# Linear attention and a squared-ReLU FFN on one core: the first phase is issued from a written table instead of by the scheduler

## The chip, the cores and the metric

The kernel runs on one core of a Trainium2 chip. The metric is device time in microseconds (us). The kernel before was run three times: 893.98, 896.58 and 896.88 us, median 896.58. The profile is of one more execution, which took 896.0 us; the span that the profile covers is 894.0 us.

## What is computed

Eight batches of eight heads, 576 positions, head size 64. In each head, q is normalised by a softmax over the head size and k by a softmax over the positions; the output is q times (k transposed times v). The outputs of the heads of one position stand side by side as 512 columns, and a feed-forward network follows.

```python
def _attn_ref(q, k, v):
    q_s = q - np.max(q, axis=-1, keepdims=True)
    q_s = np.exp(q_s)
    q_s = q_s / (np.sum(q_s, axis=-1, keepdims=True) + 1e-09)
    k_s = k - np.max(k, axis=2, keepdims=True)
    k_s = np.exp(k_s)
    k_s = k_s / (np.sum(k_s, axis=2, keepdims=True) + 1e-09)
    kv = np.einsum('bhsd,bhse->bhde', k_s, v)
    return np.einsum('bhsd,bhde->bhse', q_s, kv).astype(np.float32)

def _moe_ref(x, w_in, w_out):          # x: 4608 x 512
    h = x @ w_in                       # 512 x 2048, float64
    r = np.maximum(h, 0.0)
    return ((r * r) @ w_out).astype(np.float32)   # 2048 x 512, float64
```

## The kernel before, in words

**Work.** Heads go in pairs, four pairs to a batch, 32 pairs in all; I call them pair 0 to pair 31. The 576 positions of a batch are 512 that make a block of the FFN and 64 that are left over; the left-overs of all eight batches make a ninth block. So the FFN has nine blocks of 512 rows. A block has 16 chunks of 128 FFN columns. For each chunk the kernel forms h (`ffn_h`, L427: four parts over the 512 input columns, each three matmuls of 512 columns, L407 to L409, because every operand is split into a high and a low half), applies ReLU and the square and splits the result (`activate`, L411), and two steps later adds the chunk's product with w_out to four accumulators (`ffn_out`, L433: four parts of three matmuls, L441 to L443).

**Weights.** They arrive as float64, 512 KB a chunk, 16 chunks of w_in and 16 of w_out. `load_w` (L144) fetches one on SP's queue; `split_weight` (L153) turns it into a float32 high and low half: two ACT operations (L165 on the lowest byte, L167 into PSUM bank 3), two on DVE (L169, L170), one more on ACT (L177) and one on POOL (L178). All 32 chunks go through the same PSUM bank, one after the other.

**Attention of the first two batches** (pairs 0 to 7, the early form). Per pair: the maximum of k (L219), its transpose on PE (L223), a second maximum (L225) and its spread over the partitions (L251); k minus this, exponential (L256, L257); the same for q with a maximum per row (L261, L263, L266), its sum and division (L273 to L276); k times v on PE (L300), scaled (L308 to L316); q transposed on PE (L348, L350), copied (L353); the product (L359), split into x_hi and x_lo (L189, L190). Pairs 8 to 31 use another form, which transposes q through a bounce in DRAM (L285, L288).

**What sets the order.** The program is written unit by unit (L479 to L579): loads in the order of `LOADS` (L31), attention of batch 0 in a skewed loop (L498), h parts of the first four chunks as pairs finish, then block 0 with the attention of batch 1 in numbered slots. The framework's scheduler then decides the order on every engine from its own estimates, steered by `tc.high_priority` and `tc.issue_after`. Once built, each engine executes its own list strictly in order, and an instruction waits on semaphores of other engines or of transfers. SP issues the loads, except for q of pairs 0 and 1, which ACT issues.

**Buffers.** Four PSUM banks (`banks`) serve all uses; four more are the first phase's own (`ps_first`, L92) and later the accumulators (`ps_o`, L515). k, v and q tiles of pairs 0 to 3 are separate; from pair 4 on they share two sets (`NB = 2`, L69).

Of the kernel before, what the change touches and what calls it, by code (L numbers as in the profile page):

```python
# [42 lines left out]
def attention_ffn_kernel(ctx: ExitStack, tc: tile.TileContext, q, k, v, w_in, w_out, out):  # L43
# [48 lines left out]
    ps_first = start.enter_context(tc.tile_pool(name="ps_first", bufs=2, space=bass.MemoryType.PSUM))  # L92
# [42 lines left out]
    def load_one(b, pr, n):  # L135
        load(tiles(b, pr)[n], (k, q, v)[n], b, pr, n)

    def load_pair(b, pr):
        for n in range(3):
            load_one(b, pr, n)  # L140

    chunks, last = [], []
# [10 lines left out]
    def split_weight(part, fc):  # L153

        raw = raws[part, fc]
        low, high = raw[:, :, 0], raw[:, :, 1]
        w = w_pool.tile([P, 512], U32, name="w", bufs=WB)
        wf = w.bitcast(F32)

        with ExitStack() as order:
            if his:
                order.enter_context(tc.issue_after(his[-1].ins))
            nc.scalar.activation(low, raw.bitcast(U8)[:, :, 3], AF.Copy, scale=1 / 32, bias=-15.5 / 32)  # L165
        t = banks[3]
        nc.scalar.activation(t, high.bitcast(F32), AF.Copy, scale=2.0**-112)  # L167
        t = t.bitcast(U32)
        nc.vector.scalar_tensor_tensor(out=t, in0=t, scalar=3, in1=low, op0=ALU.logical_shift_left, op1=ALU.bitwise_or)  # L169
        nc.vector.scalar_tensor_tensor(out=w, in0=high, scalar=0x80000000, in1=t, op0=ALU.bitwise_and, op1=ALU.bitwise_or)  # L170
        finish_split()
        chunk = stay.tile([P, 2, 512], F32R, name=f"w{part}{fc}", tag=f"{part}{fc}")
        chunks.append(chunk)
        (wi if part == "i" else wo)[fc] = chunk

        def parts():
            his.append(nc.scalar.copy(chunk[:, 0], wf))  # L177
            nc.gpsimd.tensor_tensor(chunk[:, 1], wf, chunk[:, 0].bitcast(F32), op=ALU.subtract)  # L178

        unsplit.append(parts)  # L180

    his, unsplit = [], []

    def finish_split():
        while unsplit:
            unsplit.pop()()

# [4 lines left out]
    def ordered(f, *args):  # L192

        with ExitStack() as order:
            if last:
                order.enter_context(tc.issue_after(last[-1].ins))
            return f(*args)

    def attention(b, pr):

        n = b * NPAIR + pr
        i = n % NB
        kk, qq, vv = tiles(b, pr)
        kvd = kvn[i]
        early = n < EARLY
        e_q = nc.gpsimd if early else nc.vector
        st = {}
        odd = early and n % 2 == 1

        def bank(cols):  # L210
            if b == 0 and odd:
                t = ps_first.tile([P, NT], F32, name="first_ps", tag="a")
            else:
                t = next_bank("first" if b == 1 else "a") if b else banks[2]
            return t[:, :cols]

        def k_max():
            m = attn_pool.tile([P, 2, D], F32, name="m")
            nc.vector.tensor_reduce(m, kk.rearrange("p h j d -> p h d j"), axis=AX.X, op=ALU.max)  # L219
            if early:  # L220

                ps = bank(2 * P) if b else ps_first.tile([P, 2 * P], F32, name="max_ps", tag="a")
                last.append(nc.tensor.transpose(ps[:, :P], m.rearrange("p h d -> p (h d)"), ident))  # L223
                st["mc"] = attn_pool.tile([P, 1], F32, name="mc", bufs=2)
                nc.vector.tensor_reduce(st["mc"], ps[:, :P], axis=AX.X, op=ALU.max)  # L225
                st["mb"] = ps
                if b == 0:
                    k_spread()
            else:


                mt = attn_pool.tile([P, 4, BLK], F32, name="mt", bufs=1)
                nc.vector.transpose(mt, m.rearrange("p h (e a) -> p (h e) a", a=BLK))
                m1 = attn_pool.tile([P, 4], F32, name="m1", bufs=1)
                nc.vector.tensor_reduce(m1, mt, axis=AX.X, op=ALU.max)
                m4 = attn_pool.tile([BLK, 4, 4], F32, name="m4", bufs=1)
                for g in range(4):
                    nc.vector.tensor_copy(m4[:, g], m1[g * BLK : (g + 1) * BLK])  # L238
                m5 = attn_pool.tile([P, 4, 1], F32, name="m5", bufs=1)
                for g in range(4):  # L240
                    nc.vector.tensor_reduce(
                        m5[g * BLK : (g + 1) * BLK, :, 0], m4.rearrange("p g c -> p c g"), axis=AX.X, op=ALU.max
                    )
                mb = attn_pool.tile([P, 2, 1, D], F32, name="mb", bufs=1)
                nc.vector.tensor_copy(mt, m5.broadcast_to([P, 4, BLK]))
                nc.vector.transpose(mb.rearrange("p h o (e a) -> p (h o e) a", a=BLK), mt)
                st["mb"] = mb

        def k_spread():
            ps = st["mb"]  # L250
            last.append(nc.tensor.matmul(ps[:, P:], st["mc"].broadcast_to([P, P]), ident, start=True, stop=True))  # L251
            st["mb"] = ps[:, P:].rearrange("p (h o d) -> p h o d", h=2, o=1)
# [37 lines left out]
        def kv():  # L290
            ke = st["ke"]
            ps = bank(D + 1)
            for part in range(1 if b else 2):
                for j in range(LOW):
                    for h in range(2):
                        if b:
                            dst, rhs = ps[half[h], : D + 1], vv[:, h, j, :]
                        else:
                            dst, rhs = (ps[half[h], D : D + 1], ones) if part else (ps[half[h], :D], vv[:, h, j, :])
                        mm = nc.tensor.matmul(dst, ke[:, h, j, :], rhs, start=(j == 0), stop=(j == HIGH))  # L300
                        if not b:
                            continue
                        if h == 1 and j == HIGH:
                            last.append(mm)
            if b == 0 and pr < NB:
                pad_v(pr, nc.gpsimd)
# [29 lines left out]
        def q_t_early(j0, j1):  # L336
            def go():
# [13 lines left out]
                if b:  # L351
                    last.append(mm)
# [58 lines left out]
    def activate(ps, blk, fc):  # L411
# [9 lines left out]
        if blk == 0:  # L421
            his.append(gh)
# [187 lines left out]
```

## Time and profile before

| | us |
|---|---|
| runs (three) | 893.98, 896.58, 896.88; median 896.58 |
| the profiled execution | 896.0 |
| its span | 894.0 |
| PE busy in the span | 867.6 (97%) |
| DVE, ACT, POOL busy | 578.2, 408.0, 202.6 |
| first matmul of the FFN starts | 26.82 |
| as many FFN parts are done as block 0 has (64 of h, 64 of output) | 153.7 |

The span starts with the first instruction on the chip. PE's busy time counts a matmul at any clock. The granted clock is 1.00 at 2.4 GHz and 0.50 at 1.2 GHz. In a timeline row, the bracket at the end is the idle time of that engine just before the row, and what ended it. PE idles for 26.4 us of the span; what happens between 26.8 and 153.7 us, the time of block 0, is shown in the rows.

### The profile page before, as it was taken

The numbers are of one execution on the slowest core, as the hardware profiler recorded it, in microseconds if no ns is written. First come the engines' busy times: TensorE is split into PE (matmuls) and PEld (weight loads), VectorE is DVE, ScalarE is ACT, GpSimd is POOL, SyncE is SP. The second block draws the span as 40 slices with busy tenths as digits, with TensorE's granted clock in tenths as the row PEclk, the third lists the DMA queues.
The fourth block names the chain that finished last, engine by engine and source line by source line (L and its number), as shares of the span: only waits on it lengthen the run. The fifth ranks groups of instructions, "written<-read, shape, count | busy, mean of one in ns | idle before, by whom it ended". The sixth has DMA issues, their size and how long they took to land.

```text
span 894.0 us, 12672 instructions
## 1 busy us (share of the span) xinstructions
PE 867.6 (97%) x4368; PEld 702.2 (79%) x4368; DVE 578.2 (65%) x1177; ACT 408.0 (46%) x801; POOL 202.6 (23%) x177
## 2 busy tenths in 40 slices
PE   4899899999999999999999999999999999999997
PEld 3577677888888888878888888888888888888885
DVE  7768798877778776878687768886864342223222
ACT  3867766445444444554454544444444232222222
POOL 3667534222213220231122212222222000000000
PEclk9989999999999999999999999999999999999999
DMA  9897212422142313322322233222411030002001
GB/s 255 269 361 207 69 28 59 118 73 84 44 118 74 82 59 98 92 72 69 92 79 79 57 82 92 79 63 63 101 32 32 3 94 1 1 1 47 1 1 47
DMA packets 95743, 73.18 MB, mean 82 GB/s; under 512 B 47552, under 2 KB 85440, under 8 KB 95680
## 3 DMA queue, kind: packets, MB, share of 16 engines
q1 hardware_dynamic: 94944, 71.53, 28.6%
q10 hardware_dynamic: 736, 0.85, 0.4%
q8 instruction: 34, 0.56, 0.3%
q14 instruction: 29, 0.24, 0.1%
HBM read 54.00 MB, written 18.35 MB: 81 GB/s over the span
## 4 chain that ended last, share of the span: by engine, by line
PE 85%; DVE 3%; DMA 1%; issue 1%; ACT 0%; SPq 0%; DVEq 0%; ACTq 0%
PE o_ps L441 14%; PE o_ps L443 14%; PE o_ps L442 14%; PE bank L407 14%; PE bank L409 13%; PE bank L408 13%; PE bank L300 2%; PE bank L379 1%; DVE w L170 1%; DVE bank L169 0%; DVE r L417 0%; DMA kt<-in_k_dram 0%; DMA qt<-in_q_dram 0%; DVE m L219 0%; DVE m L238 0%
## 5 line engine op out<-in xcount | busy, mean ns | idle before, releaser
L407 PE MATMUL bank<-x_hi,wi 128*128 128x512 f32 x568 | 225.7, 398 | 3.0 <-ACT x_hi L189 2.2
L441 PE MATMUL o_ps<-wo,g_hi 128*128 128x512 f32 x576 | 227.4, 397 | 0.8 <-ACT g_hi L420 0.8
L442 PE MATMUL o_ps<-wo,g_hi 128*128 128x512 f32 x576 | 225.3, 391 | 0.0
L443 PE MATMUL o_ps<-wo,g_lo 128*128 128x512 f32 x576 | 224.4, 391 | 0.0
L409 PE MATMUL bank<-x_hi,wi 128*128 128x512 f32 x568 | 222.9, 392 | 0.0
L408 PE MATMUL bank<-x_lo,wi 128*128 128x512 f32 x568 | 222.6, 392 | 0.0
L419 DVE TENSOR_TENSOR r<-r 128x512 f32<-128x512 f32 x128 | 111.7, 873 | 117.2 <-ACT r L413 116.9
L424 DVE TENSOR_TENSOR g_lo<-r,g_hi 128x512 fp32r<-128x512 f32 x132 | 99.7, 755 | 105.1 <-ACT g_hi L420 102.9
L420 ACT CAST g_hi<-r 128x512 fp32r<-128x512 f32 x144 | 89.3, 620 | 129.6 <-PE o_ps L442 80.1
L413 ACT ACTIVATE r<-bank 128x512 f32<-128x512 f32 x142 | 84.6, 596 | 100.1 <-PE bank L409 95.5
L407 PEld LDWEIGHTS bank<-x_hi,wi 128*128 128x128 f32 x568 | 107.0, 189 | 27.6 <-ACT x_hi L189 3.6
L441 PEld LDWEIGHTS o_ps<-wo,g_hi 128*128 128x128 f32 x576 | 108.4, 188 | 24.3 <-ACT g_hi L420 1.0
L443 PEld LDWEIGHTS o_ps<-wo,g_lo 128*128 128x128 f32 x576 | 108.6, 188 | 22.5
L442 PEld LDWEIGHTS o_ps<-wo,g_hi 128*128 128x128 f32 x576 | 108.6, 189 | 22.3 <-POOL wo L178 0.2
L409 PEld LDWEIGHTS bank<-x_hi,wi 128*128 128x128 f32 x568 | 107.2, 189 | 23.0
L408 PEld LDWEIGHTS bank<-x_lo,wi 128*128 128x128 f32 x568 | 107.3, 189 | 21.5 <-issue 0.2
L390 POOL TENSOR_TENSOR x_lo<-xf,x_hi 128x256 fp32r<-128x256 f32 x48 | 39.5, 823 | 372.9 <-ACT x_hi L389 372.1
L333 POOL TENSOR_TENSOR qs<-qT,qs 64x640 fp32r<-64x640 f32 x48 | 82.1, 1710 | 58.4 <-ACT qs L332 47.0
L219 DVE TENSOR_REDUCE m<-kt 128x128 f32<-128x640 f32 x32 | 41.5, 1299 | 18.9 <-DMA kt<-in_k_dram 18.9
L332 ACT CAST qs<-qT 64x640 fp32r<-64x640 f32 x48 | 34.9, 726 | 37.1 <-DMA qT<-bounce 36.5
L266 ACT ACTIVATE qn<-qn 128x640 f32<-128x640 f32 x32 | 23.6, 739 | 53.5 <-DVE qn L263 46.5
L381 ACT COPY xf<-bank 64x320 f32<-64x320 f32 (+1 forms) x96 | 37.9, 394 | 20.2 <-PE bank L379 12.0
(118 smaller groups left out, 774.0 us busy)
## 6 DMA issues: line engine op xcount, KB each, us to landing
out_dram<-o SPq DMA_DIRECT2D x70, 128.0 KB, 2.3
raw_i<-in_moe_w_in_dram SPq DMA_DIRECT2D x16, 512.0 KB, 8.3
raw_o<-in_moe_w_out_dram SPq DMA_DIRECT2D x16, 512.0 KB, 9.0
bounce<-tb SPq DMA_DIRECT2D x24, 320.0 KB, 2.1
qT<-bounce SPq DMA_DIRECT2D x96, 80.0 KB, 2.2
kt<-in_k_dram SPq DMA_DIRECT2D x32, 160.0 KB, 2.9
qt<-in_q_dram SPq DMA_DIRECT2D x30, 160.0 KB, 2.9
vt<-in_v_dram SPq DMA_DIRECT2D x56, 80.0 KB, 2.5
```

The lines of the kernel that those rows point to most:

```text
L219: nc.vector.tensor_reduce(m, kk.rearrange("p h j d -> p h d j"), axis=AX.X, op=ALU.max)
L333: nc.gpsimd.tensor_tensor(qs[other], qT[own], qs[own].bitcast(F32), op=ALU.subtract)
L407: nc.tensor.matmul(ps, wi[fc][:, 0, sl], xh[:, cc, :], start=(cc == 0), stop=False)
L408: nc.tensor.matmul(ps, wi[fc][:, 0, sl], xl[:, cc, :], start=False, stop=False)
L409: last.append(nc.tensor.matmul(ps, wi[fc][:, 1, sl], xh[:, cc, :], start=False, stop=(cc == NCC - 1)))
L413: nc.scalar.activation(r, ps, AF.Relu)
L419: nc.vector.tensor_tensor(r, r, r, op=ALU.mult)
L420: gh = nc.scalar.copy(g_hi, r)
L424: e.tensor_tensor(g_lo, r, g_hi.bitcast(F32), op=ALU.subtract)
L441: nc.tensor.matmul(acc[t], g_hi[:, ts], wo[fc][:, 0], start=(n == 0), stop=False)
L442: nc.tensor.matmul(acc[t], g_hi[:, ts], wo[fc][:, 1], start=False, stop=False)
L443: prev = nc.tensor.matmul(acc[t], g_lo[:, ts], wo[fc][:, 0], start=False, stop=(n == NFC - 1))
```

## The change

The first phase, that is all loads, the attention of pairs 0 to 7, all weight chunks, block 0 of the FFN and the first half of pair 8's attention, is no longer written as loops and left to the scheduler. It is a list of 708 tokens, `FIRST`, which is issued word by word with the scheduler switched off (`tc.manual_schedule()`); every engine gets its instructions in the order of this one list. The blocks from 1 on are issued and scheduled as before, in the same slots.

A token names one operation: `Lk0a` is the first of two loads of k of pair 0 (`Lv4a` to `Lv4d` the four of v in pairs from 4 on), `Wi4` the load of chunk 4 of w_in, `wli4 wti4 wci4 wdi4 whi4 wpi4` the six steps of its split (ACT L165, ACT L167, DVE L169, DVE L170, ACT L177, POOL L178 of the kernel before), `H1.0` part 0 of h of chunk 1 (three matmuls), `r1 sq1 gh1 gl1` its activation, `O1.0` part 0 of its output. `m T mc S ks ke`, `qm qs qe sm sa rc qn`, `KV rs kn`, `TA TB ca cb`, `PX PL xh xl lf St` are the steps of a pair's attention; `@B2` or `@C0` names the PSUM bank. `X0` to `X5` are the six first steps of pair 8.

```diff
-EARLY_SPLITS = [("o",2),("o",3),("i",4),("o",0)]
-OFFSET = 100
-LOADS = "k0 q0 v0 k1 q1 v1 k2 q2 w0 v2 k3 q3 v3 w1 w2 w3".split()
-ACT_LOADS = {(0, 0, 1), (0, 1, 1)}
+ACT_LOADS = {0, 1}
+FIRST = """
+Lk0a Lq0b Lk0b Lq1a Lk1a Lq0a Lq1b Lv1b Lk1b Lk2a Lv0a m0 Lv1a Lk2b qm0 T0@C0 Lk3b mc0 Lv0b qs0 qm1 S0 Lq2b m1 Wi0
...
+O13.1 gl14 who15 O13.2 wpo15 O13.3 O14.0 gh15 O14.1 gl15 O14.2 O14.3 O15.0 O15.1 O15.2 O15.3
+""".split()
...
-    ps_first = start.enter_context(tc.tile_pool(name="ps_first", bufs=2, space=bass.MemoryType.PSUM))
+    ps_o = ctx.enter_context(tc.tile_pool(name="ps_o", bufs=4, space=bass.MemoryType.PSUM))
...
+            if name == "W":
+                load_w(part, fc)
+            elif name == "wl":
+                nc.scalar.activation(low, raw.bitcast(U8)[:, :, 3], AF.Copy, scale=1 / 32, bias=-15.5 / 32)
+            elif name == "wt":
+                nc.scalar.activation(t, high.bitcast(F32), AF.Copy, scale=2.0**-112)
...
+            if name == "H":
+                h_part(ps, 0, fc, n)
+            elif name == "r":
+                nc.scalar.activation(new(fc, "r", [P, NT], pool=work), ps, AF.Relu)
...
+        for token in FIRST:
+            if token[0] == "X":
+                steady[0][0][int(token[1:])]()
+                continue
+            name, n, part, bank = re.fullmatch(r"([A-Za-z]+)(\d+)(\.\d|[a-d])?(?:@(\w+))?", token).groups()
...
+    with tc.manual_schedule():
+        first_phase()
+    tc.no_sync_barrier()
+
+    steps = [(blk, fc) for blk in range(B + 1) for fc in range(NFC)]
...
-    for n in range(len(steps) + LAG):
+    for n in range(NFC, len(steps) + LAG):
```

The numbers of instructions by engine and kind are the same in both programs. Three places where the order differs follow; the line numbers of the second list of each are those of the changed kernel.

PE, from the pair products to the first h matmuls. `first_ps`, `early` and `bank` are PSUM tiles, `vt` and `ke` v and the exponential of k, `qT` and `qe` q transposed, `wi` a split chunk of w_in. Before:

```order
L300 MATMUL first_ps_278<-ones_93,ke_253 64x1 x2
L350 MATMUL bank2_89<-ident_96,qn_192 128x64
L300 MATMUL first_ps_278<-ones_93,ke_253 64x1 x8
L350 MATMUL first_ps_331<-ident_96,qn_245 128x64
L359 MATMUL bank2_89<-qT_95,kvn0_85 128x512
L223 MATMUL max_ps_341<-ident_96,m_339 128x128
L359 MATMUL first_ps_346<-qe_321,kvn1_86 128x512
L407 MATMUL bank0_87<-x_hi0_91,wi0_242 128x512
L251 MATMUL max_ps_341<-ident_96,mc_343 128x128
```

In the changed kernel (the numbers of the h lines become L317 to L319):

```order
L452 MATMUL early0_135<-vt1_82,ke_215 64x64 x10
L452 MATMUL early0_135<-ones_93,ke_215 64x1 x10
L472 MATMUL early1_136<-ident_96,qn_163 128x128 x4
L472 MATMUL bank2_89<-ident_96,qn_173 128x128 x4
L413 MATMUL early0_135<-ident_96,m_224 128x128
L478 MATMUL early1_136<-qT_95,kvn0_85 128x512
L478 MATMUL bank2_89<-qe_139,kvn1_86 128x512
L417 MATMUL early0_135<-ident_96,mc_299 128x128
L469 MATMUL early1_136<-ident_96,qn_163 128x64
L317 MATMUL bank1_88<-x_hi0_91,wi1_302 128x512
```

The pair products no longer interleave with the transposes, the 64-column transpose of pair 1 moves behind the first h matmuls, and the first h is of chunk 1 instead of chunk 0.

ACT, around the first weight chunks (`raw` is a chunk as loaded, `w` the rebuilt float32). Before:

```order
L165 ACTIVATE raw_i0_151<-raw_i0_151 128x512
L167 ACTIVATE bank3_90<-raw_i0_151 128x512
L257 ACTIVATE ke_253<-ke_253 128x640
L353 COPY qT_95<-bank2_89 128x512
L257 ACTIVATE ke_328<-ke_328 128x640
L177 CAST wi0_242<-w_237 128x512
L353 COPY qe_321<-first_ps_322 128x512
L353 COPY qT_95<-bank2_89 128x64
L165 ACTIVATE raw_i1_161<-raw_i1_161 128x512
L167 ACTIVATE bank3_90<-raw_i1_161 128x512
```

In the changed kernel:

```order
L502 ACTIVATE raw_i0_171<-raw_i0_171 128x512
L504 ACTIVATE bank3_90<-raw_i0_171 128x512
L465 ACTIVATE kvn0_85<-bank2_89,rs_251 64x64 x2
L502 ACTIVATE raw_i1_176<-raw_i1_176 128x512
L504 ACTIVATE bank3_90<-raw_i1_176 128x512
L518 CAST wi0_278<-w_264 128x512
L465 ACTIVATE kvn1_86<-early0_135,rs_280 64x64 x2
L476 COPY qT_95<-early1_136 128x512
L476 COPY qe_139<-bank2_89 128x512
L518 CAST wi1_302<-w_293 128x512
L502 ACTIVATE raw_i4_218<-raw_i4_218 128x512
L484 CAST x_hi0_91<-early1_136 128x512
```

The first step of a chunk's split (L165, now L502) stands further ahead of the rest of it: three chunks are begun before the first x_hi, where one was complete and one begun.

SP, the loads after those of batch 0. Before:

```order
L148 DMA raw_i1_161<-in_moe_w_in_dram 128x4x256 [waits DMAHW1_49]
L148 DMA raw_i2_163<-in_moe_w_in_dram 128x4x256 [waits DMAHW2_49]
L148 DMA raw_i3_165<-in_moe_w_in_dram 128x4x256 [waits DMAHW3_49]
L150 DMA raw_o2_167<-in_moe_w_out_dram 128x1024 [waits DMAHW4_49]
L148 DMA raw_i4_169<-in_moe_w_in_dram 128x4x256 [waits DMAHW5_49]
L150 DMA raw_o3_171<-in_moe_w_out_dram 128x1024 [waits DMAHW6_49]
L148 DMA raw_i5_173<-in_moe_w_in_dram 128x4x256 [waits DMAHW7_49]
L150 DMA raw_o0_175<-in_moe_w_out_dram 128x1024 [waits DMAHW0_49]
L148 DMA raw_i6_177<-in_moe_w_in_dram 128x4x256 [waits DMAHW1_49]
L150 DMA raw_o1_179<-in_moe_w_out_dram 128x1024 [waits DMAHW2_49]
L148 DMA raw_i7_181<-in_moe_w_in_dram 128x4x256 [waits DMAHW3_49]
L124 DMA kt0_79<-in_k_dram 64x2x320 [waits DMAHW4_49,DVE_49]
```

In the changed kernel:

```order
L185 DMA raw_i4_218<-in_moe_w_in_dram 128x4x256 [waits DMAHW6_49]
L163 DMA kt3_106<-in_k_dram 64x2x320 [waits DMAHW7_49]
L163 DMA qt3_108<-in_q_dram 64x2x320 [waits DMAHW0_49]
L185 DMA raw_i2_257<-in_moe_w_in_dram 128x4x256 [waits DMAHW1_49]
L187 DMA raw_o3_262<-in_moe_w_out_dram 128x1024 [waits DMAHW2_49]
L163 DMA qt0_83<-in_q_dram 64x2x320 [waits DMAHW3_49,Pool_49]
L185 DMA raw_i3_274<-in_moe_w_in_dram 128x4x256 [waits DMAHW4_49]
L165 DMA vt3_107<-in_v_dram 64x2x256 [waits DMAHW5_49]
L187 DMA raw_o2_296<-in_moe_w_out_dram 128x1024 [waits DMAHW6_49]
L163 DMA vt3_107<-in_v_dram 64x2x320 [waits DMAHW7_49]
L187 DMA raw_o11_309<-in_moe_w_out_dram 128x1024 [waits DMAHW0_49]
```

Weights and the tiles of batches 0 and 1 are now mixed instead of standing in runs. In both programs a load on SP waits on one of eight semaphores (DMAHW0 to DMAHW7), that is for the load eight places before it.

## Rows read from the trace of the kernel before

**Rows 1.** The page, part 1: busy us (share) and instructions.
```profile
PE 867.6 (97%) x4368; PEld 702.2 (79%) x4368; DVE 578.2 (65%) x1177; ACT 408.0 (46%) x801; POOL 202.6 (23%) x177
```
**Rows 2.** Busy time by stretch: length, then busy (instructions) by engine, granted clock, DMA, GB/s.
```profile
0.00:26.80 26.80, 15.44 (x104) 10.45 (x105) 18.77 (x44) 12.16 (x23) 11.21 (x23) 1.00 0.97 278
26.80:153.70 126.90, 117.64 (x637) 89.13 (x636) 100.03 (x191) 88.69 (x171) 73.40 (x60) 0.96 0.53 160
153.70:888.20 734.50, 734.50 (x3630) 602.64 (x3630) 458.99 (x942) 306.76 (x608) 117.99 (x94) 1.00 0.23 60
```
**Rows 3.** Groups by line on PE and DVE, 0 to 153.7 us: busy, mean ns.
```profile
L407 PE MATMUL bank<-x_hi,wi 128*128 128x512 f32 x60 | 26.0, 439 | 3.0 <-ACT x_hi L189 2.2 <-DVE r L417 0.8
L441 PE MATMUL o_ps<-wo,g_hi 128*128 128x512 f32 x60 | 24.8, 430 | 0.8 <-ACT g_hi L420 0.8
...
L300 PE MATMUL bank<-vt,ke 128*64 128x65 f32 x99 | 4.8, 228 | 0.1
...
L407 PE MATMUL h_ps<-x_hi,wi 128*128 128x512 f32 x8 | 3.1, 411 | 0.0
...
L219 DVE TENSOR_REDUCE m<-kt 128x128 f32<-128x640 f32 x11 | 14.1, 1285 | 4.9 <-DMA kt<-in_k_dram 4.9
```
**Rows 4.** Timeline of PE: start, length, instruction, idle time before and its end.
```profile
43.53 0.73 PE L407 MATMUL bank<-x_hi,wi 128*128 128x512 f32 x2 [2.21 <-ACT x_hi L189]
...
102.71 0.36 PE L223 MATMUL bank<-ident,m 128*128 128x128 f32 x1 [2.49 <-ACT kvn L314]
```
**Rows 5.** Busy time by stretch, after the two longest of these gaps.
```profile
43.50:51.50 8.00, 7.05 (x19) 5.38 (x20) 5.86 (x9) 4.02 (x8) 6.28 (x6) 0.58 0.93 301
102.70:106.70 4.00, 3.99 (x11) 3.17 (x12) 3.06 (x6) 2.50 (x5) 1.75 (x2) 0.57 0.25 74
```
**Rows 6.** Timeline of PE: pieces of attention and of h.
```profile
10.81 1.34 PE L300 MATMUL bank<-vt,ke 128*64 128x64 f32 x20 [1.74 <-ACT ke L257]
...
16.21 1.08 PE L348 MATMUL bank<-ident,qn 128*128 128x128 f32 x4
...
23.82 2.08 PE L359 MATMUL bank<-qT,kvn 128*128 128x512 f32 x2
...
26.82 1.26 PE L407 MATMUL bank<-x_hi,wi 128*128 128x512 f32 x1
...
60.94 0.80 PE L300 MATMUL bank<-vt,ke 128*64 128x65 f32 x20
...
62.23 0.40 PE L409 MATMUL bank<-x_hi,wi 128*128 128x512 f32 x1
...
64.31 0.39 PE L409 MATMUL bank<-x_hi,wi 128*128 128x512 f32 x1
...
71.19 1.02 PE L359 MATMUL bank<-qT,kvn 128*128 128x512 f32 x2
```
**Rows 7.** Timeline of DVE, the first maximum of k; timeline of SP, the ninth load.
```profile
6.07 1.23 DVE L219 TENSOR_REDUCE m<-kt 128x128 f32<-128x640 f32 x1 [3.16 <-DMA kt<-in_k_dram]
...
7.31 0.61 SPq L124 DMA_DIRECT2D kt<-in_k_dram  x1
```
**Rows 8.** DMA issues from 0 to 10 us: KB each, median us to landing; then the page's for weights.
```profile
vt<-in_v_dram SPq DMA_DIRECT2D x2, 128.0 KB, 4.3
...
raw_i<-in_moe_w_in_dram SPq DMA_DIRECT2D x16, 512.0 KB, 8.3
```
**Rows 9.** Busy time by stretch; the last two columns are the DMA share and GB/s.
```profile
0.00:20.00 20.00, 8.64 (x66) 6.25 (x67) 14.13 (x35) 7.38 (x12) 6.90 (x17) 1.00 0.93 239
20.00:32.00 12.00, 12.00 (x99) 8.12 (x101) 8.62 (x17) 8.95 (x19) 7.90 (x10) 1.00 1.06 398
...
36.00:48.00 12.00, 8.61 (x28) 4.96 (x27) 9.96 (x15) 8.90 (x20) 6.76 (x6) 0.87 0.64 171
```
**Rows 10.** Waits of SP's queue, 0 to 120 us: total, times, longest.
```profile
SPq L368 <- ACT left L367: 9.5, 3, 6.1
SPq L124 <- DVE qn L263: 5.3, 1, 5.3
```

More of the change, by code (lines that the diff above doesn't have):

```diff
@@ L81, in next_bank @@
         taken[who] += 1
-        return banks[{"first": n % 3, "h": n % 2, "a": 2 + n % 2}[who]]
+        return banks[{"h": n % 2, "a": 2 + n % 2}[who]]
     x_hi.append(moving.tile([P, NCC, NT], F32R, name="x_hi0"))
@@ L135, in load_one @@
     def load_one(b, pr, n):
[L136 to L142, printed above, removed]
+        for part in range(4 if n == 2 and b else 2):
+            load_part(b, pr, n, part)
     def load_w(part, fc):
@@ L151, in load_w @@
         raws[part, fc] = raw
[L153 to L186, printed above, removed]
     def split(hi, lo, src):
@@ L190, in split @@
         nc.vector.tensor_tensor(lo, src, hi.bitcast(F32), op=ALU.subtract)
[L192 to L197, printed above, removed]
     def attention(b, pr):
-        n = b * NPAIR + pr
-        i = n % NB
         kk, qq, vv = tiles(b, pr)
-        kvd = kvn[i]
-        early = n < EARLY
-        e_q = nc.gpsimd if early else nc.vector
         st = {}
-        odd = early and n % 2 == 1
         def bank(cols):
[L211 to L215, printed above, removed]
+            return next_bank("a")[:, :cols]
         def k_max():
@@ L219, in k_max @@
             nc.vector.tensor_reduce(m, kk.rearrange("p h j d -> p h d j"), axis=AX.X, op=ALU.max)
[L220 to L252, printed above, removed]
+            mt = attn_pool.tile([P, 4, BLK], F32, name="mt", bufs=1)
+            nc.vector.transpose(mt, m.rearrange("p h (e a) -> p (h e) a", a=BLK))
+            m1 = attn_pool.tile([P, 4], F32, name="m1", bufs=1)
+            nc.vector.tensor_reduce(m1, mt, axis=AX.X, op=ALU.max)
@@ L292, in kv @@
             ps = bank(D + 1)
[L293 to L306, printed above, removed]
+            for j in range(LOW):
+                for h in range(2):
+                    nc.tensor.matmul(ps[half[h]], ke[:, h, j, :], vv[:, h, j, :], start=(j == 0), stop=(j == HIGH))
             rs = attn_pool.tile([P, 1], F32, name="rs")
@@ L525, in attention_ffn_kernel, with open_late @@
+    def open_late():
+        start.close()
+        late = ctx.enter_context(tc.tile_pool(name="late", bufs=1))
+        x_hi.append(late.tile([P, NCC, NT], F32R, name="x_hi1"))
+        x_lo.append(late.tile([P, NCC, NT], F32R, name="x_lo1"))
+    steady = [attention(2 + i // NPAIR, i % NPAIR) for i in range((B - 2) * NPAIR)]
+    with tc.manual_schedule():
+        first_phase()
+    tc.no_sync_barrier()
+    steps = [(blk, fc) for blk in range(B + 1) for fc in range(NFC)]
     LAG = 2
```

424 lines of the change are left out of this document (259 added, 165 removed).

## The prediction

> **What bounds the kernel now.** The page's first part comes first: PE is busy 867.6 of 894.0 us and DVE, the next, 578.2 [rows 1]. A kernel with such a PE can gain only where PE stands still, works at the lower clock or waits inside small matmuls, so I cut the span into stretches [rows 2]. From 153.7 to 888.2 us PE is busy all 734.5 us: nothing is to be had there, and the change leaves that part as it is. Up to 26.8 us PE is busy 15.4 us and feeds the first pairs; from 26.8 to 153.7 us it is busy 117.6 of 126.9 us at a mean granted clock of 0.96. This second stretch is block 0, and both stretches are what the table now orders.
>
> How much work that is: by 153.7 us PE had run 60 + 8 parts of h and 60 parts of output [rows 3], 128 parts, exactly what block 0 has (four output parts of block 0 were still open, and four h parts of block 1 done in their place). A part is three matmuls; from 62.23 to 64.31 us nine take 2.08 us [rows 6], so 0.693 us a part and **88.7 us** for 128. The attention of pairs 0 to 7, priced at full clock, is near 3 us a pair: a product of k and v 0.73 (40 matmuls, so twice that, in batch 0), four transposes 0.43, the product with q 0.9, the rest 0.5 or so; these are read from starts around the rows at 60.94 and 71.19 us [rows 6]. Eight pairs make **24 us**, and the whole first phase 112.7 us of PE at 2.4 GHz.
>
> In the table 7.3 us of that stand ahead of the first h part, `H1.0`; in the order before it is about 6.9. So after the first h matmul at 26.82 us, 126.9 us passed for some 106.2 us of work (112.7 less 6.9, plus 0.7 for the first product of pair 8: 99 matmuls of 128x65 had run [rows 3], and pairs 4 to 7 have 80). **The loss is 20.7 us.** Of it 9.3 us is PE idle (126.9 less 117.6 [rows 2]), in gaps of which the largest are 2.21 and 2.49 us [rows 4], and about 5.1 us is the clock: after these two gaps the granted clock is 0.58 over 8 us and 0.57 over 4 us [rows 5], that is a large share of the time at 1.2 GHz, 8 x 0.42 + 4 x 0.43. The other 6.3 us is matmuls held up by each other: small ones between large ones, and a slow start, since the first h matmul lasts 1.26 us [rows 6].
>
> **The change, part by part.** No instruction is added or removed; only the order moves. I cost it in three terms.
>
> *The start of h.* The first maximum of k starts at 6.07 us, when its loads have landed [rows 7]; they are still SP's first two. Then three things move. The v loads of pair 0 fall back: the second is now eleventh on SP, two places behind a load that is issued at 7.31 us [rows 7]; at about 0.65 us a place it is issued at 8.6, and 4.3 us to landing [rows 8] make 12.9 us. So pair 0's product starts at about 13 instead of 10.81 us [rows 6]: 2.2 us later. The exponential of k, which DVE serves only after the maxima of pair 1, would be ready at about 12 and is covered by that wait. But from there PE runs dense: two products of 2.2 us (the one of pair 0 took from 10.81 to 13.05), eight transposes of 1.08 us for four [rows 6], then two products with q of 1.9 us (2.08 us is the pair of instructions of one [rows 6]) with small pieces between, 11.6 us in all at the clock seen there. That ends at 24.6 us. The clock row says 1.00 there [rows 2], yet the product with q takes twice the 0.9 us of later; if the denser start ends this slow time earlier, the end is at 22 to 23 us, and the longest it could be is the old 26.8. I take **24 us** for `H1.0` against 26.82: a gain of 2.8 us. ACT's x_hi of pair 0 stands behind the first step of chunk 4 of w_in; that chunk is behind some 4.5 MB, 19 us of loads at 239 GB/s [rows 9] or less, so it has landed by then.
>
> *From there to the end of block 0.* With no loss 105.4 us of work follow (112.7 less 7.3), to 129.4 us. The table removes the reason for the biggest gaps: the h parts of the first four chunks no longer wait together for one x_hi at 43.5 us, and the maximum that waits for ACT at 102.71 us [rows 4] now has banks of its own place. I can't show that each gap goes; a fixed order has gaps where a duration differs from what its author assumed. I keep **half of the 20.7 us**, 10.3 us. The block then ends at 24 + 105.4 + 10.3 = 139.7 us.
>
> *Behind block 0* nothing changes on PE. There the kernel before had 128 parts and 0.7 us of pair 8 done at 153.7 us; so the changed span is its own end of block 0 plus 894.0 - 153.7 + 0.7 = 741.0 us. With 139.7 that is 880.7 us; the profiled execution lies 2.0 us over its span and the median of the runs 0.6 us over that. **883 us**, 13 below the median.
>
> What else has to fit. ACT, DVE and POOL were busy 100.9, 118.8 and 84.6 us by 153.7 us [rows 2]; 118.8 in 139.7 us is 85% for DVE, and some of it (11 first maxima of k had run [rows 3], eight for batches 0 and 1 and three for batch 2, of which the table keeps one) moves behind block 0, where DVE is busy 459 of 734.5 us.
>
> *The loads* are the second limit. 32 chunks of 512 KB [rows 8] are 16.8 MB; where chunks dominate, the trace moves 398 GB/s at a DMA share of 1.06, and 239 where k, q and v do [rows 9]: 42.2 us for the chunks, 14.8 for batch 0's 3.5 MB, 14 for the 3.2 MB of batch 1 that stand ahead of the last chunk, in all 71 us, with start and landing **about 75 us**. The kernel before is slower than that, because SP stood waiting for left-over copies (9.5 us) and freed tiles (5.3 us) [rows 10] and the rate fell to 171 GB/s from 36 to 48 us [rows 9]. In the table the step that needs the last chunk has 57.7 us of PE work ahead of it, 50.4 behind `H1.0`: at 74 us if nothing stalls. So the loads run just as fast as PE needs them, and cost nothing in my sum beyond the half I kept.
>
> A rule speaks against that: the Trainium skill, DMA: Bandwidth & Descriptors, section Bandwidth, says that HBM binds a load at about 358 GB/s a core (and that a lone core can get more). By that figure the chunks would take an estimated 46.9 us and every later step would stand 4.7 us later, 888 us. The trace shows 398 GB/s over 12 us, so I don't take it.
>
> **Rivals.** *The plan holds nearly whole:* the gaps vanish, the end of block 0 is 129.4 to 133 us, the time 873 to 876. For it: DVE and ACT have room, and the loads fit. Against: weights are begun in landing order on ACT, so one late chunk stops the ACT work behind it.
>
> *The loss stays:* each late landing stops ACT, PE runs dry, and the 20.7 us return; then only the start is gained: 24 + 105.4 + 20.7 + 741.0 + 2.6 = 894 us, within the noise of 896.6 (0.3%, 2.7 us, is about what can be told from no change).
>
> *Slower: the mixed loads starve ACT.* SP holds eight loads, each waiting for the one eight before; with small tiles between chunks the eight carry fewer bytes, and chunks may move at the mixed rate. PE then follows the loads: 55.0 us of work behind the last chunk's step. It comes out level with before when that step is at 153.0 - 55.0 = 98 us, i.e. 23 us later than 75, when the 16.8 MB take 65 us: **258 GB/s is the point that decides**. At the 239 of the first 20 us [rows 9] they take 70.2 us, the step is at 103 us, block 0 ends at 158 and the time is 902 us. For it: 171 GB/s from 36 to 48 us; against: there SP waited for buffers, and elsewhere the share stays above 1.
>
> What the clock would add: by the rows a gap of 2.5 us costs 1.7 to 3.4 us more [rows 5]. The Trainium skill, TensorE: Matmul & The Clock Gate, Part 1, says that idling throttles the clock and activity releases it; the trace agrees (0.58 after the gap at 43.5 us).
>
> **How the numbers follow.** My forecast, a gain of about 6 to 20 us: 0.60. Plan nearly whole: 0.17. Loss mostly kept but still over 2.7 us gained: 0.09. Level: 0.06. Slower: 0.08. So faster 0.86, same 0.06, slower 0.08. The range: from no loss at all and the higher speed from the start (128 us, 871) to nearly all of the loss (893).
>
> **What would show it.** In the changed profile: first h matmul at 22 to 25 us; PE idle from there to the end of block 0 of 3 to 6 us instead of 9.3; fewer stretches with a clock near 0.58; DMA share near 1 without the hole from 36 to 48 us and the last chunk landing near 75 us; 734 us of unbroken PE behind. I'm wrong if ACT's first split steps wait for loads for more than some 10 us in total, or if PE's loss behind the first h exceeds 18 us.

## The result and the profile after

The changed kernel takes 888.18 us (median of four runs, 886.89 to 888.71), the kernel before 895.28 us beside it: a ratio of 0.9919, 95% interval 0.9893 to 0.9946. So it is faster, by 7.1 us where the forecast had 13, and inside the forecast range. The profiled execution took 888.59 us with a span of 886.6.

Part 1 of the page of the changed kernel:

```profile
PE 861.8 (97%) x4368; PEld 699.0 (79%) x4368; DVE 578.7 (65%) x1177; ACT 409.0 (46%) x801; POOL 200.9 (23%) x177
```

Its busy time by stretch (length, then busy us of PE, PE's weight loads, DVE, ACT, POOL; granted clock, DMA share, GB/s), cut at the first h matmul and at the end of block 0:

```profile
0.00:25.07 25.07, 13.75 (x102) 9.53 (x102) 17.76 (x42) 12.00 (x22) 9.69 (x21) 1.00 0.96 246
25.07:142.59 117.52, 111.41 (x619) 86.37 (x619) 91.20 (x160) 88.45 (x169) 70.15 (x60) 0.99 0.65 180
142.59:886.60 744.01, 736.62 (x3649) 603.08 (x3647) 469.77 (x976) 308.58 (x612) 121.11 (x96) 1.00 0.23 62
```

The span is 7.4 us shorter than before (894.0 to 886.6): the start gives 1.7 us, block 0 gives 8.6, and behind block 0 3.0 are lost again.

Against [rows 2], PE's idle time between the first h matmul and the end of block 0 falls from 9.3 to 6.1 us and its clock rises from 0.96 to 0.99. But behind block 0, where PE had no gap before, it now idles 7.4 us, most of it at the very end of the span as before ([rows 2] stop at 888.2 of 894.0 us) and 1.6 us right behind the block. With the prediction's 105.4 us of work, the **loss in block 0** is 142.59 - 25.07 - 105.4 = 12.1 us (20.7 before), and **the rest of the span** is 744.0 us (741.0 forecast). Taken apart as the prediction took the old loss apart, it is 6.1 us of idle time (9.3 before), about 1.7 of low clock behind the longest gap (4 x 0.42; 5.1 before) and some 4.3 of matmuls that hold each other up (6.3 before).

Where PE stands still now, from PE's timeline (start, length, instruction, idle time before and its end): the first three in block 0, the last two behind it.

```profile
55.65 0.50 PE L317 MATMUL bank<-x_hi,wi 128*128 128x512 f32 x1 [2.15 <-DVE r L538]
73.85 0.50 PE L317 MATMUL bank<-x_hi,wi 128*128 128x512 f32 x1 [0.59 <-ACT qe L476]
78.90 0.27 PE L469 MATMUL bank<-ident,qn 64*128 64x64 f32 x1 [0.68 <-DVE x_lo L486]
...
149.61 0.50 PE L317 MATMUL bank<-x_hi,wi 128*128 128x512 f32 x1 [0.45 <-ACT r L323]
...
160.25 0.64 PE L294 MATMUL bank<-qs,kvs 128*128 128x320 f32 x2 [0.70 <-DVE kvs L192]
```

The gaps of 2.21 and 2.49 us of [rows 4] are gone; one of 2.15 us is left. Behind it the clock is again near 0.58, as in [rows 5]:

```profile
55.60:59.60 4.00, 3.95 (x10) 3.12 (x11) 3.84 (x6) 3.70 (x7) 2.53 (x3) 0.58 1.08 324
```

DVE, which ended that gap, had itself stood 2.97 us for the load of k of pair 5, ahead of the `r` that PE waited for:

```profile
53.71 1.29 DVE L409 TENSOR_REDUCE m<-kt 128x128 f32<-128x640 f32 x1 [2.97 <-DMA kt<-in_k_dram]
54.90 0.69 DVE L538 TENSOR_TENSOR r<-r,bank 128x512 f32<-128x512 f32 x1
```

The waits for loads from 20 to 143 us (total us, times, longest):

```profile
DVE m L409 <- DMA kt<-in_k_dram: 8.0, 5, 3.0
ACT raw_o L502 <- DMA raw_o<-in_moe_w_out_dram: 5.0, 8, 1.2
DVE qm L427 <- DMA qt<-in_q_dram: 3.0, 3, 1.9
ACT raw_i L502 <- DMA raw_i<-in_moe_w_in_dram: 2.4, 4, 0.9
```

And the loads themselves, by stretch as above. The hole of [rows 9] is closed, since the DMA share stays above 1; but 398 GB/s is reached nowhere for long:

```profile
20.00:50.00 30.00, 28.09 (x176) 19.18 (x176) 22.69 (x40) 25.50 (x53) 16.53 (x17) 1.00 1.08 301
50.00:75.00 25.00, 21.64 (x107) 16.37 (x106) 17.22 (x29) 20.16 (x36) 16.31 (x14) 0.93 1.05 291
```

The page's part 3 (packets, MB, share of 16 engines' span) of the kernel before:

```profile
q1 hardware_dynamic: 94944, 71.53, 28.6%
```

And of the changed one. For the same bytes the queue's packets took 0.286 x 894.0 = 255.7 us there and take 0.300 x 886.6 = 266.0 us here:

```profile
q1 hardware_dynamic: 94944, 71.53, 30.0%
```

I call the place where the table ends and the scheduled blocks begin the seam. DVE behind it, from its timeline: it takes two maxima of k (pairs 9 and 10), their q maxima and 4 us more of preparation before the first square of block 1 (L326) at 151.21 us:

```profile
143.40 1.32 DVE L204 TENSOR_REDUCE m<-kt 128x128 f32<-128x640 f32 x1
144.63 0.81 DVE L231 TENSOR_REDUCE qm<-qt 128x10 f32<-128x640 f32 x1
145.36 1.29 DVE L204 TENSOR_REDUCE m<-kt 128x128 f32<-128x640 f32 x1
...
151.21 0.65 DVE L326 TENSOR_TENSOR r<-r 128x512 f32<-128x512 f32 x1
```

In the first 20 us behind block 0 DVE is busy 18.96 us and PE 18.37 (columns as above):

```profile
142.59:162.59 20.00, 18.37 (x94) 13.75 (x93) 18.96 (x50) 7.94 (x17) 3.13 (x2) 1.00 0.39 96
```

In the kernel before, from the same amount of work on, DVE is busy 15.23 us and PE all the time; there the maxima of pairs 9 and 10 were already done ([rows 3]: 11 first maxima by 153.7 us, where the table has nine):

```profile
153.00:173.00 20.00, 20.00 (x90) 16.24 (x90) 15.23 (x37) 9.92 (x21) 2.05 (x2) 1.00 0.47 121
```

The last copy of block 1's results starts 639.0 us ahead of the end of the span before and 638.8 us ahead of it now, so the 3.0 us are lost while block 1 runs. PE's idle time is 1.6 of them; the other 1.4 us are PE's busy time, 736.6 us against 735.2 before (734.5 [rows 2] and the 0.7 of pair 8), and why it grows is not explained. The two copies:

```profile
255.01 0.68 DVE L458 COPY o<-o_ps 128x512 f32<-128x512 f32 x1
```

And in the changed kernel:

```profile
247.84 0.68 DVE L364 COPY o<-o_ps 128x512 f32<-128x512 f32 x1
```

### The profile page after: what moved, and what is told of

Its sections match the earlier page's. It is cut to its first block, busy times and chain, and to the rows that moved or that the text cites. A ratio compares the mean times of both kernels' runs of the same rounds, so it can differ in the third digit from the quotient of the medians.

```text
span 886.6 us, 12646 instructions
## 1 busy us (share of the span) xinstructions
PE 861.8 (97%) x4368; PEld 699.0 (79%) x4368; DVE 578.7 (65%) x1177; ACT 409.0 (46%) x801; POOL 200.9 (23%) x177
## 3 DMA queue, kind: packets, MB, share of 16 engines
q1 hardware_dynamic: 94944, 71.53, 30.0%
## 4 chain that ended last, share of the span: by engine, by line
PE 89%; DMA 7%; DVE 2%; SPq 1%; ACT 1%; issue 0%; ACTq 0%; DVEq 0%
PE o_ps L340 14%; PE o_ps L342 14%; PE o_ps L341 14%; PE bank L317 14%; PE bank L319 14%; PE bank L318 14%; DMA kt<-in_k_dram 3%; PE bank L265 2%; PE bank L294 1%; DMA qt<-in_q_dram 1%; DMA vt<-in_v_dram 1%; DMA raw_o<-in_moe_w_out_dram 1%; DMA raw_i<-in_moe_w_in_dram 1%; PE bank L478 0%; DVE m L204 0%; SPq L165 0%
## 5 line engine op out<-in xcount | busy, mean ns | idle before, releaser
L317 PE MATMUL bank<-x_hi,wi 128*128 128x512 f32 x568 | 224.7, 396 | 3.7 <-DVE r L538 2.1
L319 PE MATMUL bank<-x_hi,wi 128*128 128x512 f32 x568 | 222.6, 392 | 0.6 <-POOL wi L521 0.6
L326 DVE TENSOR_TENSOR r<-r 128x512 f32<-128x512 f32 x128 | 109.9, 858 | 113.0 <-ACT r L323 112.5
L328 DVE TENSOR_TENSOR g_lo<-r,g_hi 128x512 fp32r<-128x512 f32 x128 | 96.9, 757 | 101.6 <-ACT g_hi L327 99.7
L327 ACT CAST g_hi<-r 128x512 fp32r<-128x512 f32 x128 | 79.4, 621 | 130.3 <-PE o_ps L341 71.9
L317 PEld LDWEIGHTS bank<-x_hi,wi 128*128 128x128 f32 x568 | 107.0, 188 | 27.9 <-DVE r L538 2.6
L340 PEld LDWEIGHTS o_ps<-wo,g_hi 128*128 128x128 f32 x576 | 108.3, 188 | 24.6 <-ACT g_hi L541 0.7
L319 PEld LDWEIGHTS bank<-x_hi,wi 128*128 128x128 f32 x568 | 106.9, 188 | 23.8 <-POOL wi L521 1.1
L323 ACT ACTIVATE r<-bank 128x512 f32<-128x512 f32 x128 | 76.3, 596 | 93.9 <-PE bank L319 92.2
L297 DVE TENSOR_TENSOR xf<-bank,xf 64x320 f32<-64x320 f32 (+1 forms) x96 | 42.8, 446 | 3.8 <-ACT xf L296 1.7
L304 ACT CAST x_hi<-xf 128x256 fp32r<-128x256 f32 x48 | 19.5, 406 | 55.1 <-DVE xf L297 54.9
```

What stands on the lines that cost most here:

```text
L297: nc.vector.tensor_tensor(x[half[h]], ps[:HALF], corr[half[h]], op=ALU.add)
L317: nc.tensor.matmul(ps, wi[fc][:, 0, sl], xh[:, cc, :], start=(cc == 0), stop=False)
L319: nc.tensor.matmul(ps, wi[fc][:, 1, sl], xh[:, cc, :], start=False, stop=(cc == NCC - 1))
L323: nc.scalar.activation(r, ps, AF.Relu)
L326: nc.vector.tensor_tensor(r, r, r, op=ALU.mult)
L327: nc.scalar.copy(g_hi, r)
```

## The experiments

All start from the changed kernel; ratios are to the kernel before, run on the same chip. "Loss" is the end of block 0 less the first h matmul less 105.4 us; "behind" is the span less the end of block 0. Both are of one profiled execution each. For the kernel before the end of block 0 is 153.7 less 0.7 us, as the prediction counted it.

| run | median us | ratio [95%] | first h | block 0 ends | loss | behind |
|---|---|---|---|---|---|---|
| before | 895.28 | | 26.82 | 153.0 | 20.7 | 741.0 |
| the change | 888.18 | 0.9919 [0.9893, 0.9946] | 25.07 | 142.59 | 12.1 | 744.0 |
| 1 no loads of batch 1 | 880.41 | 0.9825 [0.9812, 0.9838] | 25.01 | 133.53 | 3.1 | 746.0 |
| 2 weights in runs | 889.20 | 0.9923 [0.9901, 0.9946] | 24.90 | 142.68 | 12.4 | 744.9 |
| 3 halves side by side | 886.60 | 0.9900 [0.9884, 0.9915] | 26.48 | 138.27 | 6.4 | 745.0 |
| 4 scheduler on | 900.80 | 1.0058 [1.0046, 1.0070] | 27.73 | 154.00 | 20.9 | 744.9 |
| 5 no v of batch 1 | 884.03 | 0.9867 [0.9846, 0.9888] | 23.87 | 134.66 | 5.4 | 744.0 |
| 6 one maximum later | 888.58 | 0.9929 [0.9913, 0.9945] | 23.72 | 140.83 | 11.7 | 744.5 |
| 7 seam in fixed order | 890.98 | 0.9954 [0.9939, 0.9969] | 24.63 | 141.01 | 11.0 | 747.1 |
| 8 halves, later ones only | 888.55 | 0.9919 [0.9896, 0.9943] | 25.16 | 138.99 | 8.4 | 745.0 |
| 9 seam, squares first | 891.29 | 0.9952 [0.9934, 0.9971] | 24.51 | 142.12 | 12.2 | 747.3 |
| 10 long rows of v | 889.62 | 0.9939 [0.9921, 0.9957] | 23.95 | 141.66 | 12.3 | 746.3 |
| 11 seam on POOL | 889.90 | 0.9930 [0.9915, 0.9945] | 24.25 | 140.42 | 10.8 | 746.6 |
| 12 runs 3 and 11 together | 888.57 | 0.9922 [0.9904, 0.9939] | 26.76 | 141.51 | 9.3 | 745.5 |

The change and runs 7, 9 and 11 have the same operations in the same order up to the end of block 0, or nearly so; their losses are 10.8 to 12.2 us and their ends 140.4 to 142.6. The ten kernels that issue the table's first 25 loads in its order have their first h matmul at 23.7 to 25.2 us. "Behind" lies between 744.0 and 746.3 us in the nine profiles whose program behind the table is that of the change (the change and runs 1 to 6, 8 and 10). Differences of single profiles within these bounds are not told apart.

**Run 4: the table, but with the scheduler on.**

```diff
-    with tc.manual_schedule():
-        first_phase()
+    first_phase()
```

> The table stays, as the order in which the program is written, with its banks; but the scheduler may reorder again (no manual schedule). If the gain comes from issuing in a fixed order, the time goes back to 893 to 897 us and block 0 loses 18 us or more. If it comes from what the table says (bank of each operation, which step is written first), and the scheduler keeps near it, the time stays at 886 to 890 us. A scheduler free to fill gaps could also be better than the table: under 886 us.

It is slower than the kernel before. Its stretch from the first h matmul to the end of block 0:

```profile
27.73:154.00 126.27, 116.95 (x622) 88.83 (x621) 88.80 (x160) 86.40 (x167) 70.49 (x60) 0.96 0.56 163
```

126.27 us, 116.95 busy, clock 0.96: within 0.7 us of [rows 2], where the scheduler had the old program. So with the scheduler on, the table's banks and its order as a program are worth nothing; the fixed issue is worth 12.6 us against this run (900.80 to 888.18). The scheduler worked here without the `tc.high_priority` and `tc.issue_after` that steered it in the old first phase; against that steered program the gain is the 7.1 us of the change. Of the span's 12.3 us the start gives 2.7, the loss 8.8 and the rest 0.9. The stretch behind is long (744.9) with the scheduler on too, so the seam's cost does not come from the fixed issue. What both programs have is the cut itself, the barrier behind the table that keeps later work out of block 0. No run leaves the barrier out, so that it is the cause is argued and not shown.

**Runs 1 and 5: fewer loads.**

```diff
     nc.vector.memset(ones, 1.0)
+    for i in range(NB):
+        nc.gpsimd.memset(vt[i][:, 1, HIGH, HALF - 16 :], 1.0)
-... Lv4d Lq4b St0 Lv4a Wo10 Wi6 St1 Wo0 Lk4b Lk4a Wo1 Lk5a Wo15 ...
+... St0 Wo10 Wi6 St1 Wo0 Wo1 Wo15 ...
```

(run 1, SP's tokens, cut; the two memsets fill the ends of two v tiles that no load writes any more. Run 5 has the memsets too and drops `Lv4a` to `Lv7d` alone)

> Leaves out the 32 loads of k, q and v of pairs 4 to 7 (3.5 MB; pairs 4 to 7 then compute on the values of pairs 0 and 1), and nothing else. Theory L (what is left of block 0's loss comes from loads that land late): the 3.5 MB were some 12 us of loads at 290 GB/s, so the last chunk lands near 75 instead of 87 us, PE's 2.15 us gap at 55.65 us goes, block 0 ends 5 to 9 us sooner than 142.6 us, time 879 to 884. Theory O (the loss is the fixed order: small matmuls between large ones, engines that wait for one another): block 0 ends within 2 us of 142.6 us, time 886 to 889.

> Leaves out only the 16 loads of v of pairs 4 to 7 (1.18 MB of the 3.54 MB of batch 1; their rows are 256 bytes each, those of k and q 1,024 or 1,280), so these pairs use the v of pairs 0 and 1. Theory P (short rows are what makes batch 1's loads dear): most of the 9 us that leaving out all 32 loads gave comes back, block 0 ends at 137 us or sooner, time 880.5 to 884. Rival B (the bytes count): a third of it, block 0 ends at 138.5 to 141 us, time 884.5 to 887.5.

Run 1's stretch of block 0 (columns as above):

```profile
24.99:133.53 108.54, 108.21 (x619) 85.92 (x619) 91.01 (x160) 87.08 (x169) 70.18 (x60) 1.00 0.47 159
```

What is left in run 1 of DVE's waits for k:

```profile
DVE m L409 <- DMA kt<-in_k_dram: 1.2, 1, 1.2
```

PE idles 0.3 us instead of 6.1, at full clock, and 9.0 of the 12.1 us of loss are gone: theory L holds. The last chunk's issue ends at 60.4 instead of 80.3 us, so the 3.2 MB of these loads that stand ahead of it had cost 20 us. Leaving out all 3.54 MB takes 23.3 us off the queue's packet time (266.0 in the change, 0.276 x 879.5 = 242.7 here), 6.6 us a MB where the average of the queue is 3.7. Run 5 gives 4.2 of run 1's 7.8 us for a third of its bytes; its profile (the fastest of its four executions) gives more. By the medians neither of its two theories is singled out.

**Run 2: weights in runs.** SP's tokens, cut:

```diff
-... Wi5 Wi7 Lv4d Lq4b St0 Lv4a Wo10 Wi6 St1 Wo0 Lk4b Lk4a Wo1 Lk5a Wo15 St2 Wo5 ...
+... Wi5 Wi7 Wo10 Wi6 St0 St1 Lk4b Lk4a Lq4a Lq4b Lk5a Lk5b Lq5b Lq5a Wo0 Wo1 Wo15 St2 Wo5 Wi9 Wo8 Wo14 ...
```

> Only the order of SP's loads changes: weights stand in runs of 5 to 13 chunks, the k, q and v loads of batch 1 in three groups between them. Theory M (the mixing itself slows the loads): the rate from 20 to 75 us rises from about 290 to 340 GB/s or more, the last chunk lands 5 to 10 us sooner, and block 0 ends 1 to 5 us sooner, time 883 to 887. Rival B (the rate is set by what is loaded, not by its order): the rate over 20 to 75 us stays within 10 of 290 GB/s, the last chunk within 3 us of where it was, time 886 to 891.

Part 3 of the page: the queue's packet time falls back to 0.290 x 887.6 = 257.4 us, near the level of the kernel before. The five kernels with the change's load order (the change and runs 6, 7, 9 and 11) have 265.2 to 270.0 us, so the mixed order costs 8 to 13 us of it.

```profile
q1 hardware_dynamic: 94944, 71.53, 29.0%
```

But the rate from 20 to 75 us is 305 GB/s (297 in the change), short of theory M's 340, and the time is the same: the tiles now come late together. DVE's timeline has a wait of 5.11 us for q of pair 4, and PE a gap of 2.89 us behind it:

```profile
39.76 0.82 DVE L427 TENSOR_REDUCE qm<-qt 128x10 f32<-128x640 f32 x1 [5.11 <-DMA qt<-in_q_dram]
```

And SP, whose tile loads for pairs 4 and 5 stand in a row there, doesn't keep the DMA engines busy; the stretch from 36 to 44 us (columns as above) has a share of 0.68:

```profile
36.00:44.00 8.00, 5.11 (x23) 3.53 (x22) 4.00 (x6) 4.39 (x11) 2.51 (x2) 1.00 0.68 191
```

**Runs 3, 8 and 12: halves of a tile side by side.** SP's tokens, cut:

```diff
-... Lk4b Lk4a Wo1 Lk5a Wo15 St2 Wo5 Lq5b Wi9 Lk5b ...
+... Lk4b Lk4a Wo1 Lk5a Lk5b Wo15 St2 Wo5 Lq5b Lq5a Wi9 ...
```

> Only SP's order changes: the two halves of a k, q or v tile (partitions 0 to 63, and 64 to 127), which the table issues apart, stand side by side as in the kernel before. Theory H (halves apart use only half of the partitions at a time and make the loads slow): the rate from 20 to 75 us rises from about 290 to 340 GB/s or more, the last chunk lands 5 us or more sooner, time 883 to 887. Rival: the rate stays within 15 GB/s, time 886 to 890.

> As the run with the halves side by side, but only from the load of chunk 2 of w_in on; the first 25 loads stand as in the table, so the first h matmul should be back at 25.1 us (it was 26.5 there). Theory H (the later halves, issued apart, are what makes the loads land late): the rate from 50 to 75 us is again near 320 instead of 291 GB/s, block 0 ends at 136 to 138.5 us, time 883.5 to 886. Rival (the gain of that run lay in its first loads): block 0 ends within 1.5 us of 142.6 us, time 887 to 889.

In run 3 the rate from 50 to 75 us is 320 GB/s (310 in run 8, 303 in run 12), and by the waits of run 3 DVE hardly stands for k any more:

```profile
DVE m L409 <- DMA kt<-in_k_dram: 0.6, 1, 0.6
```

The loss falls to 6.4, 8.4 and 9.3 us. Part of that can be the choice of execution: the profiled one is the fastest of run 3 and the second fastest of run 8, and the second slowest of the change. Where the first loads move too (runs 3 and 12) the first h matmul comes later, at 26.5 and 26.8 us. Run 3 has the lowest median of the complete kernels, 886.60, but its interval overlaps the change's, and runs 8 and 12 show nothing in their times. That it is faster than the change isn't shown, and neither theory is singled out. In run 12 the two changes together give no gain over the change either (888.57 us).

**Run 10: the same bytes in longer rows.**

```diff
-        if n < 2 or b == 0:
+        if n < 2 or b < 2:
...
+            elif name == "CV":
+                nc.gpsimd.tensor_copy(vv[:, :, :, :D], v1[odd])
```

> v of pairs 4 to 7 is loaded in rows of 1,024 and 1,280 bytes, by two loads a pair instead of four, into two spare tiles, and POOL copies it into the padded form (four more operations, some 1.3 us each by its other 128x640 ones); the bytes are the same. Theory P (the rows of 256 bytes make the loads dear): q1's packet time falls by 4 to 10 us, block 0 ends at 135 to 139.5 us instead of 142.6, time 883 to 886. Rival B (bytes count, rows don't): block 0 ends within 1.5 us of 142.6 us, time 887 to 889.5, or later where POOL's copies hold up its split steps.

Theory P falls: by part 3 of the page 0.299 x 888.0 = 265.5 us of packet time against 266.0 (265.2 to 270.0 in the five kernels with that load order), and block 0 ends within 1 us of where it did.

```profile
q1 hardware_dynamic: 91232, 71.53, 29.9%
```

**Run 6: the maximum of pair 5 later.**

```diff
-... O2.0 Lv5c m5 r0 ... wti6 sq1 gl0 O3.0 ...
+... O2.0 Lv5c r0 ... wti6 sq1 m5 gl0 O3.0 ...
```

> One token moves: the maximum of k of pair 5, at which DVE stood 2.97 us for its load, goes behind the squares of chunks 0 and 1. Theory D (one late load stops an engine's whole list, and through it PE): the gap of 2.15 us at 55.65 us and the low clock behind it (about 1.7 us) go, block 0 ends 2 to 4 us sooner than 142.6, time 884.5 to 886.5. Rival R (what stands behind it waits for loads as well): other gaps take its place, block 0 ends within 1.2 us of 142.6, time 887 to 889.

Rival R holds by the time, and block 0 ends at 140.83 us, within what varies. The gap in PE's timeline is as long as before; PE now waits for that maximum itself:

```profile
57.45 0.33 PE L413 MATMUL bank<-ident,m 128*128 128x128 f32 x1 [2.15 <-DVE m L409]
```

**Runs 7, 9, 11 and 12: the seam.**

```diff
...
+        q_less9()
+        gs[NFC] = ffn_h(1, 0)
+        kv8()
+        gs[NFC + 1] = ffn_h(1, 1)
     tc.no_sync_barrier()
```

(run 7, inside the manual schedule; run 9 wraps the units of pairs 9 to 11 as follows)

```diff
...
+                if n in squares:
+                    order.enter_context(tc.issue_after(squares[n].ins))
+                u()
```

(run 11)

```diff
-        nc.vector.tensor_tensor(g_lo, r, g_hi.bitcast(F32), op=ALU.subtract)
+        e.tensor_tensor(g_lo, r, g_hi.bitcast(F32), op=ALU.subtract)
...
-        return activate(ps)
+        return activate(ps, nc.gpsimd if blk == 1 and fc < 8 else nc.vector)
```

> The table's order goes on over the seam: pair 9's maximum of k moves to the end of the table, and the first two h chunks of block 1 with their squares are issued in a fixed order ahead of the preparation of pairs 10 and 11. Theory S (the 3.0 us behind block 0 are DVE doing the preparation of batch 2 ahead of block 1's squares): the stretch from the end of block 0 to the end of the span shrinks from 744.0 to 741 to 742 us, PE has no gap over 0.3 us there, time 885 to 887. Rival: the 3 us come from elsewhere, the stretch stays within 0.8 us of 744.0, time 887.5 to 889.

> Only the seam: pair 9's maximum of k goes to the end of the table, and the preparation of pairs 9 to 11 is tied behind the squares of block 1 that stand two chunks ahead of its slot, so that DVE can no longer run ahead with it; nothing is issued in a fixed order behind the table. Theory S (the 3.0 us behind block 0 are DVE preparing batch 2 ahead of block 1's squares, and need only be spread): from the end of block 0 to the end of the span 741 to 742.2 us instead of 744.0, time 885 to 887. Theory C (DVE has that work to do in any case and is full there, so spreading only moves the waits, as in the run before): 743.3 us or more, time 887.5 to 891.

> In the first eight chunks of block 1 the low half of the squares is formed by POOL instead of DVE, so DVE has 8 x 0.69 = 5.5 us less to do while it prepares batch 2; everything else stays. Theory S (DVE is full behind the seam, and its backlog is the 3.0 us): from the end of block 0 to the end of the span 741 to 742.5 us instead of 744.0, DVE's square of the first chunk no longer sets PE's waits, time 885 to 887. Rival (the waits come from the order in which DVE takes its work, not from how much it has): 743.5 us or more, time 887.5 to 889.5.

> The halves side by side (as in the third run) together with the low half of the squares of block 1's first eight chunks on POOL. If the two losses are independent, the gains add: block 0 ends at 137 to 140 us, 741 to 742.5 us behind it, time 881.5 to 885. If an earlier end of block 0 only leaves DVE more to catch up, 743.5 us or more behind it and 885 to 887.

None of the three remedies shortens the stretch behind block 0: it takes 746.6 to 747.3 us in runs 7, 9 and 11 and 745.5 in run 12, which has run 11's remedy too. No median is below that of the change. In run 9 the first 20 us behind the block do become nearly dense (PE busy 19.87 us, DVE 17.57), but larger gaps stand elsewhere. From PE's timeline of run 7:

```profile
164.02 0.39 PE L294 MATMUL bank<-qs,kvs 128*128 128x256 f32 x1 [1.87 <-DVE xf L297]
```

Of run 9:

```profile
192.23 0.87 PE L265 MATMUL bank<-vt,ke 128*64 128x65 f32 x20 [2.92 <-DVE xf L297]
```

Of run 11, where the gap of 0.45 us behind the seam stays too:

```profile
157.38 0.60 PE L294 MATMUL bank<-qs,kvs 128*128 128x320 f32 x1 [1.00 <-DVE kvs L192]
```

Run 11 took work from DVE and it didn't help, but the low half takes POOL some 1.3 us instead of DVE's 0.69, and a gain could be hidden behind that. So the runs don't decide between how much DVE has to do there and in which order. Which order of DVE's work would avoid the waits stays open.

## Why the prediction was right, and where its terms were off

The forecast had the sign and the mechanism, less waiting of PE from the start of h to the end of block 0, and a gain nearly twice the measured one. Of its signs, PE's idle time in block 0 came out at 6.1 us (3 to 6 forecast), the last chunk landed at 87.4 us (75), and PE behind the block was not unbroken. By its own steps:

- *The start of h*, 24 us: measured 25.07, so 1.1 too early. The sum at the clock seen before, 24.6, was nearer; but the ten kernels with this start lie between 23.7 and 25.2 us, so the term was sound to within what varies.
- *Half of the 20.7 us is kept*, 10.3: measured 12.1, 1.8 too little. The half was a guess that no row gave, and that it came near is luck. It was kept for durations other than the author's; run 1 shows that 9.0 of the 12.1 are late loads and 3.1 everything else.
- *The loads run just as fast as PE needs them*: this step was wrong. It took 398 GB/s for chunks and 239 for tiles and added the times, last chunk near 75 us (3.2 MB at 239 GB/s are 13.4 us and not 14, so its sum is 70.4 and not 71 us; nothing hangs on that). In the mixed order all together moved at 291 to 301 GB/s, and the last chunk's issue ended at 80.3 us, with 7 us still to landing. Batch 1's tiles were put at 14 us and cost 20. The bar that was set for ACT's split steps, 10 us, was not reached (7.4 us); that DVE would wait 11.0 us for tiles had no term. By the 358 GB/s of the Trainium skill (DMA: Bandwidth & Descriptors, section Bandwidth) the estimate was 888 us, nearly the measured time, but not for that reason. From 46 to 52 us, when run 1 loads weights alone, it moves 385 GB/s (columns as above):

```profile
46.00:52.00 6.00, 6.00 (x28) 4.98 (x27) 5.37 (x8) 6.00 (x12) 5.54 (x5) 1.00 0.97 385
```

- *Behind block 0 nothing changes*, 741.0 us: measured 744.0. The prediction saw that maxima of batch 2 move behind the block and covered them with DVE's mean load there. In the first 20 us behind the seam DVE is busy 18.96, and the mean over 734 us says nothing of that. That this backlog is the whole of the 3.0 us is not shown.

1.1 + 1.8 + 3.0 = 5.9 us, the whole difference between the forecast span of 880.7 and the measured 886.6.

Of the rivals, *the plan holds nearly whole* is what run 1 shows in block 0 (loss 3.1 us, end at 133.5) once batch 1's loads are away, though its time of 880.4 us is not the 873 to 876 of that rival. *The mixed loads starve ACT* was right that the loads would land late; but DVE waited for them longer than ACT (11.0 and 7.4 us), and PE did not follow the loads to the end: from 84 us on block 0 ran without a gap.

## What to carry to other kernels

A written order can be worth having where a scheduler's own estimates decide the order on the bottleneck's engine: here the same table lost 12.6 us as soon as the scheduler was let in again, without its old steering. Once the engines' order is right, price the loads in the order in which they will be issued, not by rates read from stretches of one kind; leaving a group of loads out is a quick measure of what they cost. And a stretch with an order of its own has a seam: what the scheduler used to do ahead, across it, has to be counted against the engine's load just behind the seam, not against its mean.

## What the runs showed of the hardware that was not expected

The same 71.53 MB took 255.7 us of packet time with weights in runs, and 265.2 to 270.0 us (five profiles) mixed with tiles; setting the weights in runs again gave 257.4. Leaving out the 3.54 MB of batch 1's tiles took 23.3 us off it, 6.6 us a MB against 3.7 on average (run 1 against the change). Rows of 256 bytes or of 1,024 and 1,280 bytes for v made no difference that these runs show (266.0 and 265.5). Why mixed loads, and tiles above all, take longer was not found.
